# A linear-attention and cosine-gated MLP kernel: POOL's library load, first frames, first loads and planner durations are changed

## The chip, the cores and the metric

The kernel runs on one core of a Trainium2 chip. The metric is the device time of one execution in microseconds (us), median of three runs. The core has a matrix engine (PE, with its weight loads shown as PEld), a vector engine (DVE), a scalar engine (ACT), a general engine (POOL) and a queue engine (SP) that issues the DMA transfers here. Each engine runs its own instructions strictly in the order in which the program lists them, and waits at one whose operands are not ready; what stands behind it waits too.

## The reference

Linear attention over 8 batches of 8 heads with 576 rows of 64, then an MLP whose gate is `h * cos(h)`:

```python
q_s = softmax(q, axis=-1)            # per row, over the 64 values of a head
k_s = softmax(k, axis=2)             # per column, over the 576 rows
kv  = einsum('bhsd,bhse->bhde', k_s, v)
x   = einsum('bhsd,bhde->bhse', q_s, kv)   # -> (4608, 512)
h   = x @ w_in                       # (4608, 2048)
out = (h * cos(h)) @ w_out           # (4608, 512)
```

All of it is float32. The softmaxes subtract the maximum first, as the reference does.

## The kernel before

**Attention.** Heads are taken in pairs; batch `b` has four pairs `p`. For each pair DVE takes a maximum over the rows that lie in one partition (`k_max`, L454), POOL takes it over the 128 partitions with `partition_all_reduce` (`k_all`, L461), DVE subtracts (`k_sub`, L465), ACT takes the exponential (L471) and PE multiplies with `v` (`kv`, L483; 20 matmuls). For q two pairs are handled together, `a` = 0 or 1: `q_max` L553, `q_sub` L556, `q_exp` L560, `q_sum` L564, `q_inv` L568 and L569, `q_norm` L572. PE then transposes q (L595, L599, with the identity `ident`) and multiplies it with kv (L640), which gives x. For batch 0, x is split in high and low parts with the help of a matrix `neg` = -`ident`, which DVE makes (L236) from the identity that POOL makes with a memset and an affine select.

**MLP.** A unit `u` is one block of 512 tokens and one slice `f` of 128 of the 2048 hidden columns; there are 9 x 16 units. PE makes h in 12 matmuls (L746), ACT and DVE make the gate (L752, L756, L762, L766, L770, L774), and PE adds the product with `w_out` into four accumulators (L805, 12 matmuls). h has two buffers, so the h of unit u+2 waits for the gate of unit u (L766). The first eight slices are run for blocks 0 and 1, then the other eight, so every weight slice is needed within the first units of its turn.

**Weights.** They come as raw 64-bit words and are converted before use. One slice of `w_in` or `w_out` costs ACT `bias` L340, `bits` L345, `hi` L364 and DVE `shift` L351, `sign` L357, `lo` L368. A slice pair costs DVE six steps of 128x512.

**Order.** Nothing here is scheduled by the hardware. A `Plan` collects all steps with an engine, a duration written into the code, the tiles read and written and a due time; `Plan.order` simulates in-order engines with those durations in several rounds and returns one order, in which the instructions are then written. So each number in a `plan.add` or `plan.load` is only a cost for the planner; it changes the time through the order alone. `CFG["seq"]` fixes the order of the first loads on SP; `att1` places the due times of batch 1's attention, in units of the MLP.

**Frames.** Some tiles have borders that no load fills: `v_frame` writes ones and zeros around v, `frame` in `load_k` writes -FLT_MAX into the unused half of k's last chunk. POOL does all of them. POOL runs some of its operations from libraries that have to be loaded; the program text shows such a load as a row `ISA` without operands.

```python
ident = const.tile([P, P], F32, name="ident")
make_identity(nc, ident)
neg = const.tile([P, P], F32R, name="neg")
nc.vector.tensor_scalar_mul(neg, ident, -1.0)
```

Of the kernel before, what the change touches and what calls it, by code (L numbers as in the profile page):

```python
# [11 lines left out]
F32 = mybir.dt.float32  # L12
# [175 lines left out]
def linear_attention_then_cos_gated_mlp(  # L188
# [43 lines left out]

    ident = const.tile([P, P], F32, name="ident")
# [20 lines left out]
    def v_frame(t):  # L254
        main, last = v_parts(t)
        nc.gpsimd.memset(main[:, :, 0], 1.0)
        nc.gpsimd.memset(main[:, :, WV - 1], 1.0)
        nc.gpsimd.memset(last[D:P], 0.0)
        nc.gpsimd.memset(last[0:D, :, 0], 1.0)
        nc.gpsimd.memset(last[0:D, :, WL - 1], 0.0)  # L260
        return t
# [9 lines left out]
    plan = Plan()  # L271
    T = {}
# [40 lines left out]
    def load_w(w, f, after=0.0, seq=()):  # L313
# [14 lines left out]
        plan.load(1.46, load, writes=[R], after=after if not seq else 0.0, seq=seq)  # L328

    def convert(w, f):  # L330
# [40 lines left out]
        plan.add("ACT", 0.52, bias, writes=[R])  # L371
        plan.add("ACT", 0.52, bits, writes=[R])
        plan.add("DVE", 0.6, shift, writes=[R])
        plan.add("DVE", 0.6, sign, reads=[R], writes=[c])
        plan.add("ACT", 0.52, hi, reads=[c], writes=[R])
        plan.add("DVE", 0.6, lo, reads=[c], writes=[R])


    def load_k(b, p0, np_, tag, due, seq=()):
# [18 lines left out]
        plan.add("POOL", 0.25, frame, writes=places, due=due)  # L398
# [23 lines left out]
    def load_v(b, p, due, seq=()):  # L422
# [19 lines left out]
        if own:  # L442
            plan.add("POOL", 0.35, frame, writes=place, due=due)
# [3 lines left out]
    def k_steps(b, p, kr, vr, att, due_k, due_kv):  # L447
# [76 lines left out]
        plan.add("DVE", 0.73, k_max, reads=kr, writes=[m1], due=due_k)  # L524
        plan.add("POOL", 1.17, k_all, reads=[m1], writes=[m])
        plan.add("DVE", 0.73, k_sub, reads=[m], writes=kr)
        plan.add("ACT", 0.63, k_exp, writes=kr, table="exp")
# [3 lines left out]
        plan.add("DVE", 0.27, kv_inv, reads=[o], writes=[r])  # L531
        if b < CFG["XF"]:
            plan.add("POOL", 0.14, kv_frame, writes=[kvw], due=due_kv)
            plan.add("ACT", 0.4, kv_f32, reads=[o, r], writes=[kvw])
        else:
            plan.add("DVE", 0.33, kv_norm, reads=[o, r], writes=[kvt])
            plan.add("ACT", 0.2, kv_hi, reads=[kvt], writes=[kvw])
            plan.add("DVE", 0.2, kv_lo, reads=[kvt], writes=[kvw])
        return kvw

    def q_steps(b, a, place, due):
# [32 lines left out]
        plan.add("DVE", 1.27, q_max, reads=qr, writes=[qm], due=due)  # L574
        plan.add("DVE", 1.27, q_sub, reads=[qm], writes=qr)
        plan.add("ACT", 1.06, q_exp, writes=qr, table="exp")
        plan.add("DVE", 1.27, q_sum, reads=qr, writes=[qs])
        plan.add("DVE", 0.34, q_inv, writes=[qs])
        plan.add("DVE", 1.27, q_norm, reads=[qs], writes=qr)

    def x_steps(b, p, place, kvw, tq, tx, due_q, due_x):
# [403 lines left out]
```

## Time and profile before

| what | value |
|---|---|
| median of three runs | 916.33 us (915.85 to 916.66) |
| the profiled execution | 915.42 us, of which the span from first to last instruction is 913.6 us |
| PE busy | 867.9 us, 95% |
| DVE busy | 565.4 us, 62% |
| ACT busy | 508.6 us, 56% |
| POOL busy | 41.3 us, 5% |

Busy shares are means over the whole span. The first and last stretches differ from the rest, so the stretches have to be read apart: where PE is not busy, time is lost that PE cannot win back, since later on it is busy without a gap.

### The profile page before, as it was taken

To read this page: it belongs to the slowest core of one execution; us is meant where nothing else is said; L and a number is where in the kernel's file an instruction comes from. 1 tells how busy PE (TensorE), PEld (TensorE's weight loads), DVE (VectorE), ACT (ScalarE), POOL (GpSimd) and SP (SyncE) were. 2 spreads that over 40 slices of the span, in tenths; PEclk is the share of its full clock that TensorE was granted. 3 is DMA by queue.
4 is the path that set the end of the run, shared out by engine and by line. 5 is a ranking of instruction groups with operands and counts; after the bars stand their busy time and mean duration, and the time that the engine had idled before them with its cause. 6 is when DMAs were issued, how large, how long until landed. Compare 5 with 4: busy or idle time off the path is not lost.

```text
span 913.6 us, 11913 instructions
## 1 busy us (share of the span) xinstructions
PE 867.9 (95%) x4440; PEld 715.4 (78%) x4440; DVE 565.4 (62%) x920; ACT 508.6 (56%) x900; POOL 41.3 (5%) x84
## 2 busy tenths in 40 slices
PE   0579999999999999999999999999999999999997
PEld 0457888888888888888888888888888888888885
DVE  2998968997558654776477556845574444333332
ACT  2699778876436545574646555565563353334332
POOL 1120100000100010000000000000000000000000
PEclk9999999999999999999999999999999999999999
DMA  8573164423032011311140004100300020001001
GB/s 241 170 226 88 46 211 170 143 66 121 28 111 67 28 28 58 94 28 29 46 105 30 28 21 129 32 5 25 111 16 4 2 93 1 0 1 47 1 1 46
DMA packets 95801, 61.59 MB, mean 67 GB/s; under 512 B 53760, under 2 KB 86528, under 8 KB 95744
## 3 DMA queue, kind: packets, MB, share of 16 engines
q1 hardware_dynamic: 95744, 60.84, 22.5%
q8 instruction: 35, 0.57, 0.3%
q14 instruction: 22, 0.18, 0.1%
HBM read 48.23 MB, written 12.58 MB: 67 GB/s over the span
## 4 chain that ended last, share of the span: by engine, by line
PE 87%; DVE 6%; ACT 3%; SPq 2%; DMA 1%; issue 1%; POOL 0%; ACTq 0%; DVEq 0%
PE acc L805 41%; PE h L746 41%; PE x_False L640 2%; PE kv L483 2%; PE qt L595 1%; DVE m L454 1%; DVE k L465 1%; DMA raw_i<-in_moe_w_in_dram 1%; DMA k<-in_k_dram 1%; ACT L762 0%; ACT q L560 0%; SPq L415 0%; DVE glo L774 0%; DVE w_o L368 0%; DVE kt L766 0%
## 5 line engine op out<-in xcount | busy, mean ns | idle before, releaser
L746 PE MATMUL h<-x,w_i 128*128 128x512 f32 x1536 | 374.7, 393 | 3.3 <-DVE kt L766 3.0
L805 PE MATMUL acc<-w_o,ghi 128*128 128x512 f32 x1152 | 358.4, 392 | 0.0
L746 PEld LDWEIGHTS h<-x,w_i 128*128 128x128 f32 x1536 | 287.1, 189 | 64.6 <-DVE kt L766 3.8
L805 PEld LDWEIGHTS acc<-w_o,ghi 128*128 128x128 f32 x1152 | 213.4, 188 | 42.8
L805 PE MATMUL acc<-w_o,glo 128*128 128x512 f32 x576 | 224.5, 390 | 0.0
L756 DVE SCALAR_TENSOR_TENSOR kt<-kt,h 128x512 f32<-128x512 int32 x144 | 98.7, 686 | 142.2 <-ACT kt L752 142.0
L752 ACT ACTIVATE kt<-h 128x512 int32<-128x512 f32 x144 | 86.1, 598 | 178.2 <-PE h L746 178.0
L766 DVE TENSOR_TENSOR kt<-kt,h 128x512 f32<-128x512 f32 x144 | 98.6, 685 | 76.9 <-ACT kt L762 75.6
L770 ACT CAST ghi<-kt 128x512 fp32r<-128x512 f32 x144 | 89.5, 622 | 83.6 <-DVE kt L766 63.5
L774 DVE TENSOR_TENSOR glo<-kt,ghi 128x512 fp32r<-128x512 f32 x144 | 99.8, 693 | 56.5 <-ACT ghi L770 56.0
L805 PEld LDWEIGHTS acc<-w_o,glo 128*128 128x128 f32 x576 | 108.1, 188 | 23.3
L762 ACT ACTIVATE kt<-kt 128x512 f32<-128x512 f32 x144 | 91.3, 635 | 52.4 <-DVE kt L756 51.6
L483 PE MATMUL kv<-v_sb,k 128*64 128x66 f32 (+1 forms) x600 | 22.8, 231 | 28.7 <-ACT k L471 28.7
L483 PEld LDWEIGHTS kv<-v_sb,k 128*64 128x64 f32 x600 | 20.0, 143 | 34.7 <-ACT k L471 29.4
L746 PE MATMUL h<-x_l,w_i 128*128 128x512 f32 x192 | 46.1, 389 | 0.0
L454 DVE TENSOR_REDUCE m<-k 128x128 f32<-128x640 f32 x32 | 41.6, 1300 | 2.2 <-POOL m L461 1.5
L746 PEld LDWEIGHTS h<-x_l,w_i 128*128 128x128 f32 x192 | 36.0, 188 | 7.5
L762 ACT ACT_TABLE_LOAD x30 | 38.5, 1283 | 0.5
L461 POOL PARTITION_ALL_REDUCE m<-m x32 | 32.7, 1022 | 134.1 <-DVE m L454 126.5
L640 PE MATMUL x_False<-qt,kvw 128*128 128x288 f32 x176 | 34.6, 324 | 2.3 <-ACT qt L623 2.3
L640 PEld LDWEIGHTS x_False<-qt,kvw 128*128 128x128 f32 x176 | 28.7, 193 | 6.8 <-issue 3.1
L465 DVE TENSOR_TENSOR k<-k,m 128x640 f32<-128x640 f32 x32 | 26.5, 835 | 11.1 <-POOL m L461 11.1
(76 smaller groups left out, 550.7 us busy)
## 6 DMA issues: line engine op xcount, KB each, us to landing
raw_i<-in_moe_w_in_dram SPq DMA_DIRECT2D x16, 512.0 KB, 6.0
raw_o<-in_moe_w_out_dram SPq DMA_DIRECT2D x16, 512.0 KB, 5.4
q<-in_q_dram SPq DMA_DIRECT2D x32, 256.0 KB, 3.6
out_dram<-o SPq DMA_DIRECT2D x32, 256.0 KB, 2.3
v_sb<-in_v_dram SPq DMA_DIRECT2D x30, 256.0 KB, 3.4
k<-in_k_dram SPq DMA_DIRECT2D x14, 512.0 KB, 3.9
part<-o SPq DMA_DIRECT2D x8, 256.0 KB, 2.2
o<-part SPq DMA_DIRECT2D x8, 256.0 KB, 2.8
```

The source lines that it names most:

```text
L454: nc.vector.tensor_reduce(out=t.rearrange("p (h d) -> p h d", h=2), in_=T["k", b, p].rearrange("p h c d -> p h d c"), axis=AX.X, op=ALU.max,)
L465: nc.vector.tensor_sub(t, t, x.rearrange("p (h o d) -> p h o d", h=2, o=1).broadcast_to([P, 2, NC, D]))
L483: nc.tensor.matmul(x[h * D : (h + 1) * D, odd : odd + vt.shape[1]], t[:, h, c, :], vt, start=(c == CM), stop=(c == CM - 1),)
L640: nc.tensor.matmul(t[:, 0:HALF], a, c[:, cs], start=(n == 0), stop=(n == len(parts) - 1 and not again))
L746: nc.tensor.matmul(o, a, x, start=(c == 0 and n == 0), stop=(c == KC - 1 and n == 2))
L752: nc.scalar.activation(t, T["h", u], AF.Identity, bias=0.25, scale=1.0 / TWO_PI)
L756: nc.vector.scalar_tensor_tensor(t.bitcast(F32), t, -TWO_PI, T["h", u], op0=ALU.mult, op1=ALU.add)
L762: nc.scalar.activation(t, t, AF.Sin, bias=0.5 * math.pi)
L766: nc.vector.tensor_mul(t, t, T["h", u])
L770: nc.scalar.copy(t, T["kt", u].bitcast(F32))
L774: nc.vector.tensor_sub(t, T["kt", u].bitcast(F32), T["gh", u].bitcast(F32))
L805: nc.tensor.matmul(T["acc", j], a[:, js], w, start=(first and n == 0), stop=(last and n == 2))
```

## The change

Five edits, in the order of the program:

- Before the identity is made, DVE fills a 128x1 tile with ones and POOL runs one `partition_all_reduce` on it, whose result nobody uses. It is now POOL's first operation that needs a library.
- All frames of v, and those of k for batch 0, are written by DVE instead of POOL.
- The planner is told that POOL is taken for its first 9 us.
- The first loads come in another order: q of the first two pairs first, the first slice of `w_out` last of this list instead of second.
- Nearly all planner durations of DVE, ACT, PE and the weight loads are replaced, most of them by larger ones, and the due times of batch 1's attention are moved from units 1.29 to 3.26 to units 2.5 to 6.5.

```diff
-    att1=(1.29, 3.26),
+    att1=(2.5, 6.5),
...
     seq=[
-        ("i", 0), ("o", 0), ("v", 0), ("k", 0), ("q", 0), ("q", 1), ("k", 1), ("k", 2),
-        ("v", 1), ("q", 3), ("k", 3), ("q", 2), ("v", 2), ("v", 3),
+        ("q", 0), ("q", 1), ("k", 0), ("i", 0), ("k", 1), ("v", 0), ("q", 2), ("q", 3),
+        ("k", 2), ("v", 1), ("k", 3), ("v", 2), ("v", 3), ("o", 0),
     ],
...
+    ones, warm = (vp.tile([P, 1], F32, name=f"first{i}") for i in range(2))
+    nc.vector.memset(ones, 1.0)
+    nc.gpsimd.partition_all_reduce(warm, ones, P, RED.max)
     ident = const.tile([P, P], F32, name="ident")
     make_identity(nc, ident)
...
     def v_frame(t):
         main, last = v_parts(t)
-        nc.gpsimd.memset(main[:, :, 0], 1.0)
...
+        nc.vector.memset(main[:, :, 0], 1.0)
...
     plan = Plan()
+    plan.add("POOL", 9.0, None)
...
-            nc.gpsimd.memset(t[D:P, :, CM, :], -FLT_MAX)
+            (nc.gpsimd if b else nc.vector).memset(t[D:P, :, CM, :], -FLT_MAX)
...
-        plan.add("DVE", 0.73, k_max, reads=kr, writes=[m1], due=due_k)
-        plan.add("POOL", 1.17, k_all, reads=[m1], writes=[m])
+        plan.add("DVE", 1.28, k_max, reads=kr, writes=[m1], due=due_k)
+        plan.add("POOL", 1.05, k_all, reads=[m1], writes=[m])
```

Some thirty more lines change a duration in the same way.

The lines of the changed kernel are numbered five or six higher. On POOL the start of the program reads as follows in the kernel before, from the identity's memset to the first two all-reduces (L461) of batch 0; `v_sb` and `v` are v tiles, `kvw` the weights for x:

```order
masks.py:197 MEMSET ident 128x128
L256 MEMSET v_sb_83 128x4
L257 MEMSET v_sb_83 128x4
L258 MEMSET v_sb_83 64x132
masks.py:199 ISA
masks.py:199 AFFINE_SELECT ident<-ident 128x128
...
L506 MEMSET kvw_3_200 128x128
L461 ISA
L461 ISA m_0_226<-m_0_0_221 128x128
L461 ISA m_1_260<-m_0_1_244 128x128
```

In the changed kernel it is this, whole:

```order
masks.py:197 MEMSET ident 128x128
L512 MEMSET kvw_0_177 128x128
L237 ISA
L237 ISA first_73<-first_72 128x1
masks.py:199 AFFINE_SELECT ident<-ident 128x128
L512 MEMSET kvw_1_179 128x128
L512 MEMSET kvw_2_183 128x128
L512 MEMSET kvw_3_185 128x128
L467 ISA m_0_224<-m_0_0_218 128x128
L467 ISA m_1_241<-m_0_1_234 128x128
```

The rows without operands (masks.py:199 ISA and L461 ISA before, L237 ISA now) are the library loads: two before, one now. The first memset of kvw stands ahead of it, and no frame is filled on POOL here any more.

On DVE the first work behind the memsets of the start was this in the kernel before, as far as the first `k_sub` (L465) and what follows it; raw and wc are a weight slice in conversion, w its result:

```order
L351 SCALAR_TENSOR_TENSOR raw_i_168<-raw_i_168 128x512
L357 SCALAR_TENSOR_TENSOR wc_i_213<-raw_i_168 128x512
L351 SCALAR_TENSOR_TENSOR raw_o_176<-raw_o_176 128x512
L236 TENSOR_SCALAR neg<-ident 128x128
L454 TENSOR_REDUCE m_0_0_221<-k_0_170 128x128
L368 TENSOR_TENSOR w_i_219<-wc_i_213,w_i_219 128x512
L357 SCALAR_TENSOR_TENSOR wc_o_228<-raw_o_176 128x512
L465 TENSOR_TENSOR k_0_170<-k_0_170,m_0_226 128x640
L368 TENSOR_TENSOR w_o_232<-wc_o_228,w_o_232 128x512
L553 TENSOR_REDUCE qm_0_240<-q_0_205 128x18
```

In the changed kernel, behind 28 memsets:

```order
L559 TENSOR_REDUCE qm_0_213<-q_0_172 128x18
L460 TENSOR_REDUCE m_0_0_218<-k_0_175 128x128
L241 TENSOR_SCALAR neg<-ident 128x128
L562 TENSOR_TENSOR q_0_172<-q_0_172,qm_0_213 128x1152
L357 SCALAR_TENSOR_TENSOR raw_i_207<-raw_i_207 128x512
L471 TENSOR_TENSOR k_0_175<-k_0_175,m_0_224 128x640
L460 TENSOR_REDUCE m_0_1_234<-k_1_181 128x128
L570 TENSOR_REDUCE qs_0_239<-q_0_172 128x18
L559 TENSOR_REDUCE qm_1_256<-q_1_215 128x18
```

`neg` (L241) now stands ahead of the first `q_sub` (L562), and the conversion of the first weights has moved behind the attention of batch 0.

Later on DVE, where the k of batch 1 is first touched, the kernel before had other work between the two maxima (L454) of one load:

```order
L454 TENSOR_REDUCE m_1_0_451<-k_0_378 128x128
L491 TENSOR_SCALAR r_3_466<-kv_3_424 128x1
L494 RECIPROCAL r_3_466<-r_3_466 128x1
L357 SCALAR_TENSOR_TENSOR wc_i_472<-raw_i_266 128x512
L351 SCALAR_TENSOR_TENSOR raw_o_343<-raw_o_343 128x512
L454 TENSOR_REDUCE m_1_1_497<-k_0_378 128x128
```

The changed kernel has:

```order
L363 SCALAR_TENSOR_TENSOR wc_o_420<-raw_o_262 128x512
L497 TENSOR_SCALAR r_3_427<-kv_3_407 128x1
L500 RECIPROCAL r_3_427<-r_3_427 128x1
L460 TENSOR_REDUCE m_1_0_442<-k_0_346 128x128
L460 TENSOR_REDUCE m_1_1_476<-k_0_346 128x128
L357 SCALAR_TENSOR_TENSOR raw_i_268<-raw_i_268 128x512
```

The two maxima share one buffer (`m1` has one), and now stand directly one behind the other; they also stand earlier, ahead of nearly all weight conversions.

On DVE, from the first `k_sub` (before) or the first `q_sub` (now) up to the `lo` of the seventh slice of `w_in` (f = 6), the same steps stand in another order, but for these: only before, the first `q_max`; only now, three `shift`, `sign` and `lo` of slice 0 of `w_in`, `shift` and `sign` of slice 0 of `w_out`, and `shift` of `w_in` slice 7 and of `w_out` slice 6, seven conversion steps in all. On PE the x of pair 2 of batch 1 (4 matmuls) now stands ahead of the h of unit 6, and before stood behind it. After the first units PE's order differs in a few rows of each batch, up to the last batch of attention; from there to the end the orders of PE, ACT and DVE are the same.

## Rows read from the trace of the kernel before

**Rows 1.** Four stretches: us; PE, PEld, DVE, ACT, POOL busy (count); PEclk, DMA share, GB/s.

```profile
0.00:23.08 23.08, 0.00 (x1) 0.00 (x1) 6.60 (x13) 5.73 (x8) 4.28 (x35) 1.00 0.87 241
21.43:96.00 74.57, 56.72 (x358) 43.46 (x359) 69.55 (x108) 62.67 (x129) 9.22 (x14) 0.98 0.56 159
96.17:121.94 25.77, 25.53 (x131) 20.42 (x129) 22.86 (x38) 19.20 (x35) 4.28 (x5) 1.00 0.19 59
121.94:907.00 785.06, 785.06 (x3952) 651.35 (x3952) 467.86 (x766) 420.77 (x729) 23.56 (x30) 1.00 0.18 54
```

**Rows 2.** POOL in order of time, 0 to 40 us: start, duration, what [idle before].

```profile
1.08 0.20 POOL L258 MEMSET v_sb<- 64x132 f32 x1
...
10.19 0.28 POOL masks.py:199 TENSOR_SCALAR_AFFINE_SELECT ident<-ident 128x128 f32<-128x128 f32 x1 [8.90 <-issue]
...
13.12 0.34 POOL L506 MEMSET kvw<- 128x128 f32 x2
20.67 0.72 POOL L461 PARTITION_ALL_REDUCE m<-m  x1 [7.21 <-issue]
25.36 1.73 POOL L461 PARTITION_ALL_REDUCE m<-m  x1 [3.97 <-DVE m L454]
```

**Rows 3.** DVE in order of time, the rows around three places.

```profile
10.50 0.23 DVE L236 TENSOR_SCALAR neg<-ident 128x128 fp32r<-128x128 f32 x1 [2.71 <-POOL ident masks.py:199]
11.33 1.24 DVE L454 TENSOR_REDUCE m<-k 128x128 f32<-128x640 f32 x1 [0.60 <-POOL k L388]
...
21.43 0.83 DVE L465 TENSOR_TENSOR k<-k,m 128x640 f32<-128x640 f32 x1 [7.53 <-POOL m L461]
...
22.77 1.35 DVE L553 TENSOR_REDUCE qm<-q 128x18 f32<-128x1152 f32 x1
24.04 1.23 DVE L454 TENSOR_REDUCE m<-k 128x128 f32<-128x640 f32 x1
...
71.79 0.68 DVE L756 SCALAR_TENSOR_TENSOR kt<-kt,h 128x512 f32<-128x512 int32 x1
72.39 0.69 DVE L351 SCALAR_TENSOR_TENSOR raw_i<-raw_i 128x512 int32<-128x512 int32 x1
...
95.32 0.68 DVE L368 TENSOR_TENSOR w_i<-wc_i,w_i 128x512 fp32r<-128x512 f32 x1
```

**Rows 4.** PE in order of time: the first kv, x of batches 0 and 1, h of units 6 and 10.

```profile
23.08 1.36 PE L483 MATMUL kv<-v_sb,k 128*64 128x66 f32 x20 [23.08 <-ACT k L471]
...
36.97 2.26 PE L640 MATMUL x_False<-qt,kvw 128*128 128x288 f32 x4 [1.84 <-ACT qt L623]
...
91.97 1.13 PE L640 MATMUL x_False<-qt,kvw 128*128 128x288 f32 x4
92.72 0.84 PE L805 MATMUL acc<-w_o,ghi 128*128 128x512 f32 x2
...
96.17 3.02 PE L746 MATMUL h<-x,w_i 128*128 128x512 f32 x12
...
121.94 3.06 PE L746 MATMUL h<-x,w_i 128*128 128x512 f32 x12 [0.24 <-DVE kt L766]
```

**Rows 5.** The chain that ended last: one unit's h at full pace (start, us, what).

```profile
146.76 2.72 PE h L746 x12
```

**Rows 6.** One DMA issue on SP in order of time.

```profile
3.26 0.60 SPq L393 DMA_DIRECT2D k<-in_k_dram  x1
```

**Rows 7.** Busy time in three stretches of 10 us; columns as in rows 1.

```profile
10.00:20.00 10.00, 0.00 (x0) 0.00 (x0) 2.75 (x4) 0.62 (x1) 2.86 (x26) 1.00 0.85 225
20.00:30.00 10.00, 2.58 (x40) 2.33 (x40) 7.94 (x10) 3.88 (x7) 2.82 (x3) 1.00 0.74 207
50.00:60.00 10.00, 9.57 (x74) 7.21 (x75) 9.93 (x15) 9.22 (x24) 3.19 (x5) 1.00 0.76 241
```

**Rows 8.** DMA issues, 25 to 60 us: what, count, KB each, median us to landing.

```profile
k<-in_k_dram SPq DMA_DIRECT2D x2, 512.0 KB, 4.7
```

**Rows 9.** ACT in order of time: the first exponential of k.

```profile
22.29 0.74 ACT L471 ACTIVATE k<-k 128x640 f32<-128x640 f32 x1 [7.69 <-DVE k L465]
```

More of the change, by code (lines that the diff above doesn't have):

```diff
@@ L255, in v_frame @@
         main, last = v_parts(t)
-        nc.gpsimd.memset(main[:, :, 0], 1.0)
[L257 to L260, printed above, removed]
+        nc.vector.memset(main[:, :, 0], 1.0)
+        nc.vector.memset(main[:, :, WV - 1], 1.0)
+        nc.vector.memset(last[D:P], 0.0)
+        nc.vector.memset(last[0:D, :, 0], 1.0)
+        nc.vector.memset(last[0:D, :, WL - 1], 0.0)
         return t
@@ L326, in load @@
                 )
-        plan.load(1.46, load, writes=[R], after=after if not seq else 0.0, seq=seq)
+        plan.load(1.66, load, writes=[R], after=after if not seq else 0.0, seq=seq)
     def convert(w, f):
@@ L370, in convert @@
         c = ring("wc")
[L371 to L376, printed above, removed]
+        plan.add("ACT", 0.67, bias, writes=[R])
+        plan.add("ACT", 0.65, bits, writes=[R])
+        plan.add("DVE", 0.68, shift, writes=[R])
+        plan.add("DVE", 0.68, sign, reads=[R], writes=[c])
+        plan.add("ACT", 0.62, hi, reads=[c], writes=[R])
+        plan.add("DVE", 0.69, lo, reads=[c], writes=[R])
     def load_k(b, p0, np_, tag, due, seq=()):
@@ L396, in load @@
             nc.sync.dma_start(t[0:NL, :, CM, :], src[:, NM:S, :].rearrange("h p d -> p h d"))
-        plan.add("POOL", 0.25, frame, writes=places, due=due)
+        plan.add("POOL" if b else "DVE", 0.25, frame, writes=places, due=due)
         plan.load(0.91 * np_, load, writes=places, due=due, parts=2, seq=seq)
@@ L442, in load_v @@
         if own:
-            plan.add("POOL", 0.35, frame, writes=place, due=due)
+            plan.add("DVE", 0.45, frame, writes=place, due=due)
         plan.load(0.91, load, writes=place, due=due, parts=2, seq=seq)
@@ L572, in q_norm @@
             nc.vector.tensor_mul(rows(), rows(), over_d(T["qs", b, a]))
[L574 to L579, printed above, removed]
+        plan.add("DVE", 1.35, q_max, reads=qr, writes=[qm], due=due)
+        plan.add("DVE", 1.35, q_sub, reads=[qm], writes=qr)
+        plan.add("ACT", 1.16, q_exp, writes=qr, table="exp")
+        plan.add("DVE", 1.35, q_sum, reads=qr, writes=[qs])
+        plan.add("DVE", 0.44, q_inv, writes=[qs])
+        plan.add("DVE", 1.35, q_norm, reads=[qs], writes=qr)
     def x_steps(b, p, place, kvw, tq, tx, due_q, due_x):
@@ L697, in x_steps @@
             plan.add(
-                "ACT" if twice else "DVE", (0.37, 0.3)[i] - 0.08 * twice, lambda i=i: x_lo(i),
+                "ACT" if twice else "DVE", (0.45, 0.38)[i] - 0.04 * twice, lambda i=i: x_lo(i),
                 reads=[o, xr[2 * i]], writes=[xr[2 * i + 1]],
@@ L858, in out_rows @@
             plan.load(0.73, fetch, reads=[("part", b, j)], writes=[s])
-            plan.add("DVE", 0.6, take, reads=[acc[j]], writes=[s])
+            plan.add("DVE", 0.69, take, reads=[acc[j]], writes=[s])
         else:
-            plan.add("ACT", 0.48, take, reads=[acc[j]], writes=[s])
+            plan.add("ACT", 0.59, take, reads=[acc[j]], writes=[s])
         plan.load(0.73, put, reads=[s], writes=[("part", b, j)] if cont else [])
```

50 lines of the change are left out of this document (25 added, 25 removed).

## Prediction

> **What bounds the kernel now.** I read the busy time by stretches first. From 121.94 us to 907 us PE is busy 785.06 of 785.06 us, in a stretch in which DVE is busy 60% and ACT 54% [rows 1]. The chain of work that ended last runs through PE alone there, one unit's 12 matmuls in 2.72 us [rows 5]. So nothing that the planner does there is worth anything unless it opens a gap, and what a change wins or loses is how early PE reaches that unbroken stretch. Its first matmul, the kv of pair 0, starts at 23.08 us [rows 4]: all of the first 23.08 us is lost to PE, at a DMA share of 0.87. Between 21.43 and 96.00 us DVE is busy 69.55 of 74.57 us, ACT 62.67 and PE 56.72 [rows 1]: DVE sets the pace of this stretch, and PE follows it. At 96.00 us DVE ends the `lo` of the seventh w_in slice (95.32 + 0.68) [rows 3] and at 96.17 PE begins the h of unit 6 with it [rows 4]. From there PE has nearly no gap (25.53 of 25.77 us) [rows 1].
>
> Then the order of time on POOL and DVE shows what fills the first 23 us. POOL is idle for 8.90 us ahead of the identity's affine select and 7.21 us ahead of its first all-reduce, both put down to "issue", that is, to nothing it waited for [rows 2]. These are the places of the two rows of library loading. All frames come behind the first gap; so DVE's first maximum over k, at 11.33 us, waited for POOL's frame of k, and the first subtraction of k, at 21.43 us, waited 7.53 us for the all-reduce behind the second gap [rows 3]. The exponential follows at 22.29 [rows 9] and kv at 23.08.
>
> **Term 1: the start of the DVE stretch.** POOL reaches its one library load when the identity's memset and one memset of kvw are done; before, as many small memsets ended at 1.28 us (1.08 + 0.20) [rows 2], and the list is shorter now, so 1.1 us. The load costs between 7.2 us (the gap before the same operation, later in the program) and 8.9 us (the gap at the same place, for another operation) [rows 2]. The one is the same code, the other the same moment, so I take the middle, 8.05: done at 9.15, bounds 8.3 to 10.0. The idle all-reduce over one column takes 0.72 us as the shortest row near has it, or up to 1.0 (the rows of all 32 have a mean of 1.02, one here 1.73) [rows 2]; I take 0.85. The affine select 0.28 and `neg` 0.23 follow. `neg` now stands ahead of the first `q_sub` on DVE, so that one starts at 9.15 + 0.85 + 0.28 + 0.23 = 10.5 us, bounds 9.5 and 11.5. What stands ahead of `neg`, 28 memsets, `q_max` 1.35 and `k_max` 1.24, is hidden below this as long as the first q and k have landed: SP issues one DMA in 0.60 us and a little [rows 6], so that k, fifth and sixth, is issued by 4 us; with 4.7 us to landing [rows 8] it is there by some 8.5, and its maximum is done by 9.8. The memsets cost nothing under the wait for these loads; without that cover they would cost some 3 us.
>
> The Trainium skill ("GPSIMD Engine Reference", section 2.1) says that the first call of a freshly loaded kernel pays about 6 us for loading, with no instruction in the profile to show it. The trace agrees on the invisible gap and not on its size, 7.21 and 8.90 us; by 6 us, `neg` would wait for the k maximum instead, the first `q_sub` would start near 10.0, and the total would come out 0.5 us lower than mine.
>
> The all-reduce of pair 0 is on time: POOL is free of the affine select at 10.3, three memsets of kvw take 0.5 (two took 0.34 [rows 2]) and the all-reduce 0.72 to 1.0, so 11.5 to 11.8; DVE reaches `k_sub` at 10.5 + 1.27 + 0.60 = 12.4. The first kv then starts at 12.4 + 0.83 + 0.74 + gaps, 14.1 us, against 23.08.
>
> **Term 2: the DVE stretch itself.** From the first `k_sub` (before) or the first `q_sub` (now) to the `lo` of w_in slice 6 DVE has the same steps but for the first `q_max`, which is gone from it, and seven conversion steps of 128x512, which are new in it. Back to back, `q_max` takes 1.27 us (22.77 to 24.04) and a step of 128x512 0.60 (71.79 to 72.39) [rows 3]. So the stretch takes 74.57 - 1.27 + 7 x 0.60 = 77.5 us, if its waits are as before (74.57 - 69.55 = 5.0 us [rows 1]). It ends at 10.5 + 77.5 = 88.0 against 96.00: 8.0 us earlier.
>
> **Term 3: waits that are new in it.** The two k maxima of one load of batch 1 stand back to back and share a buffer, so the second waits for POOL's all-reduce: 0.72 to 1.73 us, I take 1.0. The first of them stands earlier in DVE's row than before: by the steps ahead of it DVE is there at about 31.5 us (21 us after the first `q_sub`). Its load cannot be issued until the second transpose of batch 0's q has left the tile, which by the chain q_norm, transposes, kv, x ends at about 25.5; SP issues it behind the store of the first x_left, at about 26. Landing 4.7 us later [rows 8] it would be in time. But the queue is deep: 8.4 MB (12 loads of q, k, v of 0.295 MB, seven weight slices of 0.52, two v and this k) come up to and with this load. In the first 20 us transfers ran at 225 to 241 GB/s [rows 1, 7], which was all that SP's issue asked for; at 50 to 60 us 241 GB/s came at a share of 0.76, that is, 317 at full share [rows 7]. With 241 GB/s from 2.2 us, where the first bytes come, to 18.5, where the weights are next (3.9 MB), and the rest at 317: 18.5 + 4.5 / 0.317 = 32.7. Between landing in time and this I take a wait of 1.0 us; bounds 0 and 7 (233 GB/s throughout: 2.2 + 8.4 / 0.233 = 38.3).
>
> **Term 4: PE.** It has the x of pair 2 of batch 1 behind it when unit 6 begins; before, that came after. 0.75 us (91.97 to 92.72) [rows 4]. Between units 6 and 10 PE took 25.77 us for eight times 12 matmuls, two x, one kv and one transpose, 8 x 2.72 + 2 x 0.75 + 1.2 = 24.5 at full pace; what of the 1.3 is won back I leave in the range.
>
> The new durations of the planner, apart from the order, run on no engine and cost nothing. Behind unit 10 they move a few rows of PE per batch, beside an unbroken PE: nothing, while DVE and ACT have over a third of the stretch free. Without that cover a gap costs what it is long.
>
> **Sum.** 8.0 - 1.0 - 1.0 + 0.75 = 6.8 us earlier. The profiled execution took 915.42 us (913.6 of span and 1.8 around it); 908.6 with the change. The median is 0.9 above that execution, so 916.33 - 6.8 = **909.5 us**.
>
> **Rivals.**
> *The transfers give the lead back.* The weights and the k of batch 1 are now asked for some ten us earlier, behind the same loads. Speaking for it: a share of 0.85 to 0.87 in the first 23 us already. Against it: between 21.43 and 96 us the share is 0.56 [rows 1]. At a wait of 2 to 5.5 us in place of 1.0 the gain is 5.8 to 2.3: 910.5 to 914.0 us.
> *The waits shrink too.* Batch 0's q is normalized before any weight is converted, so the first x, at 36.97 us before [rows 4], could come some 14 us earlier (10.5 + 8.5 for the rows to `q_norm`, then 3 for transposes and kv); if half of the 5.0 us of DVE waits and the 1.3 of PE go with it and no new ones come, the gain is 9 to 12: 904.3 to 907.3.
> *The change doesn't do what it says.* If the affine select needed a library of its own at run time, 7.2 to 8.9 us more would stand ahead of `neg`, and DVE with everything behind it: a gain of -0.4 to -2.1, 916.7 to 918.4, no change or just more. The program shows no second load there.
> *Slower: the load of batch 1's k is the new head of the chain.* DVE stops in its row at that maximum, with almost all weight conversions behind it. Each us beyond 31.5 + 1.0 costs one. It eats the gain of 6.8 when k lands at 39.3, and decides for slower by over 0.2% (1.8 us) at 41.1, which means a mean of 8.4 / (41.1 - 2.2) = 216 GB/s up to there. The stretches at 225 and 207 [rows 7] are on both sides of that, but neither had a full queue. At 207 it lands at 42.8: 3.5 slower, 919.8.
>
> **How the numbers follow.** I give the forecast (gain 5.8 to 9) 0.55, the transfers giving back 0.20, the waits shrinking 0.13, no effect 0.05, slower 0.07. 0.2% is 1.8 us, about what a measurement of this kernel can tell from no change. Faster is the first three: 0.88. The forecast's own range is 907.3 to 910.5. The range for 8 in 10 reaches into both neighbours: 904.5 to 914.0, which leaves out the last two cases and the far end of the third.
>
> **What would show it.** Right: one idle gap of POOL of 7.2 to 8.9 us near 1 to 10 us and none ahead of the all-reduce of batch 0; `neg` at 9.3 to 11.3; first kv at 13 to 15.5; the w_in `lo` of slice 6 ending near 89; PE without a gap from about there. Wrong: DVE idle for several us at batch 1's first k maximum, released by a DMA; a second POOL gap ahead of the affine select; or PE gaps after unit 10 that were not there.

## The result and the profile after

| | before | after |
|---|---|---|
| median | 916.09 us (915.27 to 916.66, 4 runs) | 908.08 us (907.75 to 910.19, 4 runs) |
| profiled execution | 915.42 us, span 913.6 | 907.75 us, span 906.0 |
| ratio after to before | | 0.9918, 95% interval 0.9901 to 0.9935 |

The change makes the kernel faster by 8.0 us (medians) or 7.7 us (profiled executions); the forecast was 6.8. The number came out, but one price inside its first term, the 8.05 us of the library load, was wrong by its whole size, and the wait for batch 1's k was wrong by 3.6 us the other way.

Busy time in four stretches of the changed kernel, with the columns of [rows 1]:

```profile
0.00:13.55 13.55, 0.00 (x1) 0.00 (x1) 8.04 (x35) 4.27 (x5) 3.46 (x12) 1.00 0.76 195
8.67:89.76 81.09, 59.81 (x365) 44.02 (x365) 72.21 (x114) 66.49 (x138) 11.37 (x15) 0.94 0.64 193
89.76:114.20 24.44, 24.44 (x125) 19.76 (x125) 23.20 (x36) 18.53 (x35) 3.08 (x4) 1.00 0.38 112
114.20:906.00 791.80, 785.53 (x3953) 651.17 (x3951) 464.22 (x767) 419.01 (x726) 21.18 (x31) 1.00 0.18 53
```

From unit 10 to the end the kernel takes 791.80 us, before 913.6 - 121.94 = 791.66: nothing changed there. All of the gain lies ahead of unit 10. DVE's stretch to unit 6 has 81.09 - 72.21 = 8.9 us of idle time where it had 5.0 [rows 1].

POOL in order of time in the changed kernel, answering [rows 2]:

```profile
0.89 0.20 POOL L512 MEMSET kvw<- 128x128 f32 x1
1.23 0.36 POOL L237 PARTITION_ALL_REDUCE first<-first  x1
1.47 0.36 POOL masks.py:199 TENSOR_SCALAR_AFFINE_SELECT ident<-ident 128x128 f32<-128x128 f32 x1
...
8.72 1.86 POOL L467 PARTITION_ALL_REDUCE m<-m  x1 [6.46 <-DVE m L460]
```

The gap of 7 to 9 us that was to be left is not there at all. The first all-reduce runs at 1.23 us, and POOL's next idle time has a releaser: it waits for DVE.

DVE in order of time, the rows that answer to [rows 3] and the two that wait longest behind them:

```profile
8.54 0.21 DVE L241 TENSOR_SCALAR neg<-ident 128x128 fp32r<-128x128 f32 x1
8.67 1.35 DVE L562 TENSOR_TENSOR q<-q,qm 128x1152 f32<-128x1152 f32 x1
11.30 0.69 DVE L357 SCALAR_TENSOR_TENSOR raw_i<-raw_i 128x512 int32<-128x512 int32 x1 [1.27 <-ACT raw_i L351]
11.91 0.82 DVE L471 TENSOR_TENSOR k<-k,m 128x640 f32<-128x640 f32 x1
...
35.63 1.29 DVE L460 TENSOR_REDUCE m<-k 128x128 f32<-128x640 f32 x1 [4.59 <-DMA k<-in_k_dram]
37.76 1.29 DVE L460 TENSOR_REDUCE m<-k 128x128 f32<-128x640 f32 x1 [0.83 <-POOL m L467]
...
89.53 0.69 DVE L374 TENSOR_TENSOR w_i<-wc_i,w_i 128x512 fp32r<-128x512 f32 x1
```

The first k subtraction comes 9.52 us earlier (21.43 to 11.91). Then DVE stands 4.59 us at batch 1's first k maximum. SP issued that k at 27.99 us, and loads of this size took 7.0 us to land (issue on SP; issues from 20 to 40 us with the columns of [rows 8]):

```profile
27.99 0.38 SPq L399 DMA_DIRECT2D k<-in_k_dram  x1
```

```profile
k<-in_k_dram SPq DMA_DIRECT2D x2, 512.0 KB, 7.0
```

What is left at the `lo` of w_in slice 6 is 5.8 us (96.00 to 90.22). PE, answering [rows 4]; the h rows are a quarter of unit 0 and those of units 2, 6 and 10:

```profile
13.55 1.35 PE L489 MATMUL kv<-v_sb,k 128*64 128x66 f32 x20 [13.55 <-ACT k L477]
...
21.14 2.29 PE L646 MATMUL x_False<-qt,kvw 128*128 128x288 f32 x4
...
42.49 1.65 PE L752 MATMUL h<-x,w_i 128*128 128x512 f32 x3
...
55.22 4.70 PE L752 MATMUL h<-x,w_i 128*128 128x512 f32 x12 [5.47 <-DVE kt L772]
...
89.76 3.08 PE L752 MATMUL h<-x,w_i 128*128 128x512 f32 x12 [0.17 <-DVE kt L772]
...
114.20 2.88 PE L752 MATMUL h<-x,w_i 128*128 128x512 f32 x12
```

The first kv is 9.53 us earlier, the first x 15.8, unit 6 6.41 and unit 10 7.74. Of the lead of 9.5 us at the start a third is lost by unit 6, and a little is won back behind it.

The 12 matmuls of unit 2 took 4.70 us behind 5.47 us without work, those of unit 10 took 2.88. The windows show where PE's clock was lower, and what filled the time before:

```profile
20.00:30.00 10.00, 9.52 (x74) 6.95 (x76) 9.86 (x17) 8.43 (x21) 2.57 (x4) 1.00 1.03 332
30.00:40.00 10.00, 8.02 (x50) 5.12 (x46) 4.32 (x7) 7.13 (x23) 2.08 (x4) 1.00 1.08 374
...
42.00:46.00 4.00, 3.82 (x37) 2.74 (x34) 4.00 (x6) 3.35 (x7) 1.49 (x1) 0.60 0.48 107
50.00:60.00 10.00, 4.78 (x14) 3.79 (x15) 10.00 (x16) 9.54 (x15) 0.00 (x0) 0.66 0.59 180
```

From 20 to 40 us the transfers run at a full share, and from 30 to 40 us DVE is busy only 4.32 of 10 us. The granted clock has a mean of 0.60 from 42 to 46 us and of 0.66 from 50 to 60 us, that is, the engine stood on the lower of its two levels, 1.2 GHz instead of 2.4, for a part of each. What the second costs is not new. Unit 2 was as slow in the kernel before:

```profile
66.39 4.62 PE L746 MATMUL h<-x,w_i 128*128 128x512 f32 x12 [2.48 <-DVE kt L766]
```

New is the first: three matmuls of unit 0, a quarter of it, took 1.65 us there, and its quarters took 0.96 to 1.08 us in the kernel before.

### The profile page after: what moved, and what is told of

It is laid out like the page before. It is cut to its first block, busy times and chain, and to the rows that moved or that the text cites. A ratio compares the mean times of both kernels' runs of the same rounds, so it can differ in the third digit from the quotient of the medians.

```text
span 906.0 us, 11877 instructions
## 1 busy us (share of the span) xinstructions
PE 869.8 (96%) x4440; PEld 714.9 (79%) x4440; DVE 564.1 (62%) x945; ACT 505.3 (56%) x898; POOL 37.2 (4%) x61
## 4 chain that ended last, share of the span: by engine, by line
PE 89%; DVE 4%; SPq 2%; DMA 2%; issue 1%; ACT 0%; POOL 0%; DVEq 0%; POOLq 0%
PE acc L811 42%; PE h L752 42%; PE x_False L646 2%; PE kv L489 2%; PE qt L601 1%; DMA v_sb<-in_v_dram 1%; DMA k<-in_k_dram 1%; SPq L421 0%; DVE m L460 0%; SPq L417 0%; DVE wc_i L363 0%; DVE k L471 0%; DMA q<-in_q_dram 0%; DVE w_o L374 0%; POOL m L467 0%
## 5 line engine op out<-in xcount | busy, mean ns | idle before, releaser
L768 ACT ACT_TABLE_LOAD x29 | 37.2, 1283 | 0.5
L467 POOL PARTITION_ALL_REDUCE m<-m x32 | 30.6, 956 | 121.9 <-DVE m L460 121.9
L624 ACT CAST qt<-qt 128x512 fp32r<-128x512 f32 (+1 forms) x36 | 15.4, 465 | 21.6 <-PE qt L601 21.6
```

The source lines that it names most:

```text
L467: nc.gpsimd.partition_all_reduce(t, T["m1", b, p], P, RED.max)
L768: nc.scalar.activation(t, t, AF.Sin, bias=0.5 * math.pi)
```

## The experiments

The theory after the first look (A in most of the expectations): the gain is the start without POOL's two gaps, carried to unit 6 by DVE's full row, less what DVE then waits for batch 1's k. The rival was that the loads' order and the planner's new numbers do it. A second question was why the one library load that is left costs nothing.

Two numbers go with each run: PE's idle time in the first 130 us (130 less PE's busy time in that window) and the mean granted clock in the same window. Each ratio is to runs of the kernel before that were timed beside it: their median was 914.52 us for e1 to e4, 915.00 for e5 to e8 and 915.77 for e9 to e12, so runs of different groups are compared by their ratios.

| kernel | median us | ratio to before (95%) | PE idle to 130 us | clock to 130 us |
|---|---|---|---|---|
| before | 916.09 | | 39.5 | 0.99 |
| after | 908.08 | 0.9918 (0.9901 to 0.9935) | 30.0 | 0.96 |
| e1 library part alone | 904.94 | 0.9893 (0.9878 to 0.9908) | 28.7 | 0.99 |
| e2 after, old numbers | 907.84 | 0.9924 (0.9912 to 0.9937) | 30.1 | 0.96 |
| e3 after, two loads | 908.30 | 0.9928 (0.9914 to 0.9941) | 31.8 | 0.96 |
| e4 after, iota at the end | 907.15 (one run) | | 29.6 | 0.96 |
| e5 after, k early | 908.67 | 0.9928 (0.9916 to 0.9941) | 31.1 | 0.95 |
| e6 after, old first loads | 906.05 | 0.9899 (0.9884 to 0.9914) | 31.7 | 0.97 |
| e7 frames alone | 912.13 | 0.9969 (0.9958 to 0.9981) | 37.2 | 0.99 |
| e8 replanned | 905.45 | 0.9895 (0.9881 to 0.9908) | 27.2 | 0.96 |
| e9 after, second xl | 909.85 | 0.9940 (0.9925 to 0.9955) | 30.9 | 0.93 |
| e10 e5 with second xl | 906.78 | 0.9907 (0.9890 to 0.9923) | 30.9 | 0.99 |
| e11 after, late weights | 907.12 | 0.9910 (0.9895 to 0.9924) | 28.5 | 0.97 |
| e12 e8 with second xl | 905.86 | 0.9895 (0.9880 to 0.9910) | 27.6 | 0.96 |

**e1: the library part alone.**

```diff
+    ones, warm = (vp.tile([P, 1], F32, name=f"first{i}") for i in range(2))
+    nc.vector.memset(ones, 1.0)
+    nc.gpsimd.partition_all_reduce(warm, ones, P, RED.max)
     ident = const.tile([P, P], F32, name="ident")
```

> The kernel before with the idle all-reduce ahead of the identity, and nothing else: old numbers, old order of the first loads, frames on POOL. Theory A (the whole gain is a start without POOL's two gaps, of 8.90 and 7.21 us, carried to unit 6 by DVE's full row, less what DVE then waits for batch 1's first k): no gap of 7 to 9 us on POOL; the first k subtraction when k has landed, its maximum and the all-reduce are done, at 10.5 to 12 us instead of 21.43; of these 9.5 to 11 us 2 to 6 are lost again to transfers, so 4 to 8 us faster than before, 908 to 912 us. Theory B (the gain hangs on the loads' new order and on the planner's new numbers, the library part alone gives little, since the first k and q come behind two weight slices): under 3 us faster, 913 us or more. PE unbroken from unit 6 on in both.

Three lines won 9.6 us by medians, 914.52 less 904.94, where the whole change won 8.0 (ratios 0.9893 and 0.9918, whose intervals just overlap). DVE's and PE's rows in order of time:

```profile
10.68 0.81 DVE L468 TENSOR_TENSOR k<-k,m 128x640 f32<-128x640 f32 x1
...
36.25 1.30 DVE L457 TENSOR_REDUCE m<-k 128x128 f32<-128x640 f32 x1
```

```profile
85.47 3.02 PE L749 MATMUL h<-x,w_i 128*128 128x512 f32 x12
...
111.22 3.06 PE L749 MATMUL h<-x,w_i 128*128 128x512 f32 x12 [0.22 <-DVE kt L769]
```

Against the kernel before the first k subtraction is 10.75 us earlier, unit 6 10.70, unit 10 10.72 [rows 3, 4], the span 10.4. The row of before has moved as a block. The new waits that theory A charged here, 2 to 6 us, did not come: batch 1's k maximum starts at 36.25 without a wait, since this order has eight conversion steps of DVE between 26 and 36 us where the changed kernel has three. The maximum itself is no earlier than in the changed kernel (35.63); what differs is how much of the later work is done ahead of it. Theory A's best case, 908 us, was 3 us short; theory B falls.

**e2: the planner's old numbers.** The changed kernel with the old durations, old due times of batch 1 and without POOL's 9 us.

```diff
-    att1=(2.5, 6.5),
+    att1=(1.29, 3.26),
...
-    plan.add("POOL", 9.0, None)
```

> The changed kernel with the planner's old durations, the old bounds for batch 1 and no 9 us of POOL; the first all-reduce, the frames on DVE and the new order of the loads stay. Theory A: the new numbers are worth nothing for the start; they set how many conversion rows DVE has ahead of batch 1's first k maximum. By its order five more of them stand ahead of it here, about 3 us of the 4.6 us that DVE waits there in the changed kernel: 905 to 908 us, the same as the changed kernel's 908.1 or 1 to 3 us faster. Theory B (durations of the trace give the planner a better order): 909.5 to 913 us, slower than the changed kernel by 1.5 us or more.

907.84 us, the same as the changed kernel: the new numbers are worth nothing that can be measured. The wait for k is gone, which is more than was expected, but DVE stands instead behind ACT, 1.33 us for w_out's `hi` and 1.80 for w_in's:

```profile
31.95 0.69 DVE L371 TENSOR_TENSOR w_o<-wc_o,w_o 128x512 fp32r<-128x512 f32 x1 [1.33 <-ACT w_o L367]
...
36.55 0.69 DVE L371 TENSOR_TENSOR w_i<-wc_i,w_i 128x512 fp32r<-128x512 f32 x1 [1.80 <-ACT w_i L367]
```

e1 and e2 were timed beside the same runs of before, and their intervals do not overlap: given the library part, frames on DVE and the new order of loads together cost 2.9 us.

**e3: two loads again.** The changed kernel without its idle all-reduce.

```diff
-    ones, warm = (vp.tile([P, 1], F32, name=f"first{i}") for i in range(2))
-    nc.vector.memset(ones, 1.0)
-    nc.gpsimd.partition_all_reduce(warm, ones, P, RED.max)
```

> The changed kernel without its idle all-reduce, so that POOL again needs a library for the affine select and another for the all-reduces. Theory A (the libraries cost what the gaps show and stand on the path): gaps of about 8.9 us ahead of the affine select and 7.2 us ahead of the first all-reduce; first k subtraction near 19 us instead of 11.91; of these 7 us DVE gives back up to 3 at the wait for batch 1's k (4.6 us now), so 4 to 7 us slower than the changed kernel: 912 to 915 us. Theory B (the gain came from the order of loads and the planner): within 1.5 us of the changed kernel, 907 to 909.5 us.

POOL, and DVE at the first k subtraction and batch 1's first k maximum:

```profile
8.40 0.28 POOL masks.py:199 TENSOR_SCALAR_AFFINE_SELECT ident<-ident 128x128 f32<-128x128 f32 x1 [7.31 <-issue]
...
15.56 0.72 POOL L464 PARTITION_ALL_REDUCE m<-m  x1 [6.43 <-issue]
```

```profile
16.31 0.83 DVE L468 TENSOR_TENSOR k<-k,m 128x640 f32<-128x640 f32 x1 [4.16 <-POOL m L464]
...
35.94 1.28 DVE L457 TENSOR_REDUCE m<-k 128x128 f32<-128x640 f32 x1 [0.81 <-DMA k<-in_k_dram]
```

Both gaps are back and the first k subtraction is 4.4 us late, yet the time is within 0.1% of the changed kernel's. At batch 1's k maximum DVE is 0.31 us behind it: its wait there fell from 4.59 to 0.81. All other instructions stand in the changed kernel's order. In this order, 4.4 us of the start are worth next to nothing, because the landing of that k decides: taken out of the whole change, the library part costs nothing that can be measured. Theory B's number came, for theory A's reason: the gaps stand where they were expected, and the k wait absorbs them, by 3.8 us where "up to 3" was granted.

**e4: another library at the end.** One iota behind everything, whose output nobody uses.

```diff
+        last = vp.tile([P, 1], I32, name="last")
+        nc.gpsimd.iota(last, pattern=[[0, 1]], base=0, channel_multiplier=1)
```

> The changed kernel with one more instruction on POOL behind all others, an iota over one column, for which POOL must load the first library; its output is used by nobody. Theory A (in the changed kernel the all-reduce's library is still there from the execution before, and so its load costs nothing): now each execution begins with the other library, and a gap of 7 to 9 us stands ahead of the first, idle all-reduce, which ends near 9 to 10 us; first q subtraction near 10.5 us instead of 8.67, first k subtraction 12 to 12.5 instead of 11.91; time 907.5 to 909.5 us, since DVE waits for raw_i and batch 1's k anyway. Theory B (a load that stands first is hidden behind the start of the program or costs nothing): no gap, the first q subtraction at 8.6 to 8.8 us, time as the changed kernel.

```profile
7.23 0.38 POOL L237 PARTITION_ALL_REDUCE first<-first  x1 [6.17 <-issue]
...
8.90 1.88 POOL L467 PARTITION_ALL_REDUCE m<-m  x1 [0.60 <-DVE m L460]
...
622.70 0.13 POOL L959 IOTA last<- 128x1 int32 x1 [6.93 <-issue]
```

Now the gap is there, 6.17 us ahead of the very instruction that ran at 1.23 us in the changed kernel, and 6.93 us ahead of the iota. So the load costs nothing in the changed kernel because the library is still there from the execution before; the kernel before used two in turn and had to load both each time. Theory A is shown for the gap. Its size of 6.17 us is below the range that I took from [rows 2]. At this size `neg` waits for the k maximum and not for POOL: it starts at 8.71 us, 0.17 later than without the gap, and the first k subtraction is only 0.03 later:

```profile
11.94 0.82 DVE L471 TENSOR_TENSOR k<-k,m 128x640 f32<-128x640 f32 x1
```

The Trainium skill ("GPSIMD Engine Reference", section 2.1) gives about 6 us for the first call of a freshly loaded kernel; 6.17 us agrees with it, and the other gaps of these runs, 6.43 to 9.40 us, are longer. One run, 907.15 us: no loss that it could show.

**e5: k ahead in the queue.** On SP only, five transfers change places: w_in 3, v(1,1), w_out 2, the store of x_left and k(1,0) in the changed kernel, and now k(1,0) ahead of the other four. The helper that finds the loads is left out here.

```diff
+    moved = [
+        load_of("load_k", (1, 0)), load_of("w", ("i", 3)), load_of("load_v", (1, 1)), load_of("w", ("o", 2))
+    ]
...
+    steps = [i for i in first if i not in moved] + moved + [i for i in steps[at + 1 :] if i not in moved]
```

> The changed kernel with one thing moved on SP: the load of batch 1's first k stands right behind the weights of w_out slice 1, ahead of w_in slice 3, the second v of batch 1, w_out slice 2 and the first store of x_left, which follow it in their old order. Theory A (the wait for this load, 4.6 us in the changed kernel, is what keeps it behind the kernel with the library part alone): k issued as soon as POOL has written its frame, near 24.8 us instead of 28; DVE waits under 1 us for it; its pair's second maximum then waits for POOL, whose row has a frame and a memset of kvw ahead of the all-reduce that end at 33.4 us, so it starts near 34.3 instead of 37.76: 2 to 3.5 us faster than the changed kernel, 904.5 to 906.5 us. Theory B (other waits stand right behind this one, so that its length doesn't decide): the first maximum comes early, and units 2 to 6 at the same times as in the changed kernel; 907 to 909 us.

DVE and ACT:

```profile
32.37 1.27 DVE L460 TENSOR_REDUCE m<-k 128x128 f32<-128x640 f32 x1 [0.25 <-DMA k<-in_k_dram]
...
39.06 0.69 DVE L357 SCALAR_TENSOR_TENSOR raw_i<-raw_i 128x512 int32<-128x512 int32 x1 [2.62 <-ACT raw_i L351]
```

```profile
35.99 0.21 ACT L663 COPY xl<-x_False 128x64 f32<-128x64 f32 x1 [3.16 <-DMA x_left<-xl]
```

The wait for k is gone and the time is not. The store of x_left went out 3.16 us later (30.57 instead of 27.41), ACT stood behind it, and DVE behind ACT. Theory B's outcome, through a wait that neither named: with one buffer for xl, the later store cost here what the earlier load had won. PE's clock has a part in the time too: units 2 and 4 took 5.49 and 4.62 us (4.70 and 3.38 in the changed kernel).

**e6: the old order of first loads** in the changed kernel.

```diff
-        ("q", 0), ("q", 1), ("k", 0), ("i", 0), ("k", 1), ("v", 0), ("q", 2), ("q", 3),
+        ("i", 0), ("o", 0), ("v", 0), ("k", 0), ("q", 0), ("q", 1), ("k", 1), ("k", 2),
```

> The changed kernel with the first loads in the order of the kernel before: w_in and w_out slice 0 first, then v, k, q. Library, frames on DVE, new planner's numbers stay. Theory A (the new order is the part that costs: with the weights first, DVE has conversions to do while q and k come, and reaches batch 1's k with work behind it): 904 to 906.5 us, near the 904.9 of the library part alone. Theory B (the new order is what gives q and k early, and the planner's new numbers cost): 909 to 912 us, slower than the changed kernel.

906.05 us, in theory A's range; 0.0019 below the changed kernel, with intervals that overlap a little. Together with e2 it points to a new order that costs and does not gain. Neither run shows that alone: this interval overlaps, and e2 differs from e1 in the frames too. The estimates are 1.7 us (from e6) and at most 2.9 (from e2).

**e7: the frames alone,** on the kernel before.

```diff
-        nc.gpsimd.memset(main[:, :, 0], 1.0)
+        nc.vector.memset(main[:, :, 0], 1.0)
...
-            nc.gpsimd.memset(t[D:P, :, CM, :], -FLT_MAX)
+            (nc.gpsimd if b else nc.vector).memset(t[D:P, :, CM, :], -FLT_MAX)
```

> The kernel before with one part of the change, the first frames on DVE; two libraries as before, old order, old numbers. Theory A (POOL's second gap begins when POOL reaches the first all-reduce; the frames between the two gaps held it back): the second gap follows the affine select at once, first k subtraction at 16.5 to 18.5 us instead of 21.43, and DVE's full row carries this to unit 6: 3 to 5 us faster than before. Theory B (26 memsets on POOL cost what they take, some 2 us, beside waits): under 1 us faster.

POOL's gaps were 9.40 us ahead of the affine select and 6.54 ahead of the all-reduce at 17.75; the first k subtraction came at 18.51 us, 2.92 earlier than before, and the kernel was 0.31% faster, 2.9 us: just short of theory A's 3 to 5 us, and theory B falls. The start's lead went one to one into the total here too.

```profile
18.51 0.82 DVE L465 TENSOR_TENSOR k<-k,m 128x640 f32<-128x640 f32 x1 [5.01 <-POOL m L461]
```

**e8: replanned.** Library and frames as in the changed kernel, the planner's old durations without POOL's 9 us, batch 1 later, a longer landing, and another order of the first loads.

```diff
-    att1=(2.5, 6.5),
+    att1=(3.5, 5.5),
...
-        return self.LAT.get((a[0], b[0]), 1.0 if a[0] == "BUS" else 0.2)
+        return self.LAT.get((a[0], b[0]), 2.2 if a[0] == "BUS" else 0.2)
```

> Library first and frames on DVE as in the changed kernel, with the planner's old durations; it is told that a transfer lands 2.2 us behind its last byte instead of 1.0, batch 1 is due later (3.5, 5.5), and the first loads come as w_in 0, k 0, q 0, q 1, v 0, k 1, w_out 0, then as in the changed kernel. Theory A (what is lost in the changed kernel behind the start are waits of DVE for transfers that the planner takes for landed): DVE waits under 1 us for batch 1's k, has its first conversion before 6 us, and unit 6 begins at 81 to 84 us: 900.5 to 904 us. Theory B (ACT or PE bounds the stretch to unit 6 as soon as DVE doesn't): 904.5 to 908 us, with DVE's idle time behind ACT.

DVE waits no more for batch 1's k, and PE's idle time is the least of all, 27.2 us; but unit 6 begins at 88.30 us and not at 81 to 84, and the time is e1's and in theory B's range. DVE does wait for ACT, three times between 31 and 37 us, 1.02 us at the longest. What the order won in idle time against e1, 1.5 us, is not in the time, and PE's matmuls were slower: the granted clock from 50 to 60 us was 0.51, and unit 2's 12 matmuls took 5.49 us (4.60 in e1).

```profile
54.36 5.49 PE L748 MATMUL h<-x,w_i 128*128 128x512 f32 x12 [2.45 <-DVE kt L768]
```

**e9 to e12: a second buffer for xl,** alone (e9), with e5's order (e10) and in e8's plan (e12); e11 changes two planner numbers instead. In e9 and e10 the planner is not told of the buffer, so that its order stays.

```diff
-        x4k=8, kq=2, qm=1, qs=2, ql=1, m1=1, m=2, r=2, kvt=1, kvw=4, xl=1, stage=2, wc=1, r2=3, ghi=2,
+        x4k=8, kq=2, qm=1, qs=2, ql=1, m1=1, m=2, r=2, kvt=1, kvw=4, xl=2, stage=2, wc=1, r2=3, ghi=2,
...
```

> The changed kernel with a second buffer for xl, the tile whose store to x_left ACT waits for; every engine's order is the changed kernel's. In the changed kernel ACT waits 1.62 and 1.12 us for these stores at 33.4 and 39.7 us, while DVE waits 4.59 us for batch 1's k. Theory A (k's late landing, not the store, holds DVE in the changed kernel): ACT's two waits go and DVE's stays; 907 to 908.5 us, as the changed kernel. Theory B (the store is part of what holds DVE): 1 us or more faster, under 907 us.

ACT's waits for the store are gone, DVE's for k is 4.24 us: theory A. But 909.85 us is outside its range, with every engine's order the same (the ratio's interval still overlaps that of the changed kernel). In the profiled executions, 2.9 us apart, the difference is in PE's clock: the 12 matmuls of unit 1 took 3.88 us and those of unit 4 5.67 (2.92 and 3.38 in the changed kernel), the mean to 130 us is 0.93.

```profile
35.55 1.31 DVE L460 TENSOR_REDUCE m<-k 128x128 f32<-128x640 f32 x1 [4.24 <-DMA k<-in_k_dram]
```

```profile
48.09 3.88 PE L752 MATMUL h<-x,w_i 128*128 128x512 f32 x12
...
75.39 5.67 PE L752 MATMUL h<-x,w_i 128*128 128x512 f32 x12
```

> Both together: batch 1's first k loaded ahead of the same four transfers as in e5, and a second buffer for xl, so that the store, which comes later for that, keeps nobody waiting. In e5 DVE waited 0.25 us for k and yet the time stayed, with ACT 3.16 us behind the store and DVE 2.62 us behind ACT. Theory A (two waits stand behind each other, for k and for the store; only with both gone is the lead kept): DVE's waits between 31 and 41 us come to under 2.5 us (5.4 in the changed kernel), units 2 to 6 start 2 to 3.5 us earlier: 904 to 906 us. Theory B (POOL's and PE's rows hold the second maximum anyway, and DVE's row behind it is set by ACT's conversions): 907 us or more.

```profile
31.30 1.27 DVE L460 TENSOR_REDUCE m<-k 128x128 f32<-128x640 f32 x1
34.46 1.30 DVE L460 TENSOR_REDUCE m<-k 128x128 f32<-128x640 f32 x1 [1.88 <-POOL m L467]
35.68 0.68 DVE L357 SCALAR_TENSOR_TENSOR raw_i<-raw_i 128x512 int32<-128x512 int32 x1
```

With the wait for this k and the one for the store gone, DVE's idle time between 31 and 41 us is 3.0 us (5.4 in the changed kernel, under 2.5 expected). DVE is at the raw_i step 3.28 us earlier than in the changed kernel (38.96 there) and unit 6 begins 3.1 us earlier, at 86.64. The time is 906.78 us, 0.8 above theory A's range: of the 3.1 us, which are still there at unit 10, 1.1 are lost behind it, most of them at one wait of PE:

```profile
120.32 3.01 PE L752 MATMUL h<-x,w_i 128*128 128x512 f32 x12 [0.92 <-DVE kt L772]
```

Against e9, which has the same buffers and was timed beside the same runs of before, the intervals do not overlap: 3.1 us faster. Against the changed kernel (0.9907 and 0.9918) the difference is not resolved.

> The changed kernel with two of the planner's numbers altered: weights may be asked for 20 us ahead of their unit instead of 28.78, and a transfer lands 2.2 us behind its last byte instead of 1.0. By its order three weight slices stand ahead of batch 1's first k on SP's queue behind w_in 0 (w_out 0, w_in 1 and 2) instead of six. Theory A (the wait for this k comes from the weights ahead of it in a full queue): 1.6 MB less ahead, at 330 to 370 GB/s 4.2 to 4.8 us: DVE waits under 1 us for k; 903.5 to 906 us. Theory B (k lands late because it is issued late, when batch 0's q has left its tile): wait of 3 us or more as now, 907 us or more.

```diff
-    wwin=28.78,
+    wwin=20,
...
-        return self.LAT.get((a[0], b[0]), 1.0 if a[0] == "BUS" else 0.2)
+        return self.LAT.get((a[0], b[0]), 2.2 if a[0] == "BUS" else 0.2)
```

```profile
30.65 1.28 DVE L460 TENSOR_REDUCE m<-k 128x128 f32<-128x640 f32 x1 [1.21 <-DMA k<-in_k_dram]
```

The k maximum starts five us earlier than in the changed kernel, so the weights ahead of that k did hold it. They held its issue: SP issued it at 23.06 us instead of 27.99, and DVE's wait for it ends 7.6 us behind the issue in both. The time is 907.12 us, which is theory B's. The planner's new order puts other rows behind it: unit 6 begins at 89.14, 0.6 us earlier than in the changed kernel, and the granted clock is 0.66 from 50 to 60 us.

> The replanned kernel of e8 with a second buffer for xl, known to the planner. Theory A (what keeps e8 at the time of the library part alone are ACT's waits and the lower granted clock behind PE's idle time at 50 to 60 us, 0.51 there): with a free ACT row PE's idle time before 130 us falls from 27.2 to 25 to 26.5 us and the clock there is higher: 902 to 904.5 us, the fastest of all. Theory B (e8's stores keep nobody waiting, ACT's row shows none of these waits): as e8, 904.8 to 906.2 us.

905.86 us, as e8: theory B. ACT had none of these waits in e8 to lose.

The fastest kernels are e1, e8, e12 and e6, which these runs do not tell apart. e1 is the kernel before with three lines more.

## Why the prediction was right, step by step

- **Its own signs.** The number is right; the signs that were named for it are mixed. The POOL gap of 7.2 to 8.9 us did not come and `neg` started at 8.54 us, ahead of its 9.3 to 11.3; the first kv (13.55), the missing gap ahead of batch 0's all-reduce and PE's unbroken row did come. And one of the signs named for "wrong" came: DVE idle for several us at batch 1's first k maximum, released by a DMA.
- **Term 1, the start: wrong by the load.** The step "the load costs between 7.2 us and 8.9 us" measured 0: the library was resident (e4). First q subtraction 8.67 us (forecast 10.5, bounds 9.5 to 11.5), set by q's landing and the maxima; first k subtraction 11.91 (12.4), first kv 13.55 (14.1). The bounds came from two rows of the same program, and both rows were of loads that replace another library; that there might be nothing to replace was not among the cases. The idle all-reduce took 0.36 us (0.85 taken).
- **Term 2, the stretch: right in its work, short in its waits.** Forecast 77.5 us with 5.0 of waits, plus 2.0 of term 3: 79.5. Measured from 8.67 to 90.22: 81.5. DVE's idle time to unit 6 is 8.9 us instead of 7.0, so its busy time is the 72.5 us of the forecast within 0.2.
- **Term 3, the new waits: the k wait mis-sized.** 1.0 us was taken, bounds 0 and 7; it was 4.59. DVE was there at 31.04 as forecast (31.5), the k was issued at 27.99 instead of 26, and it took 7.0 us to land instead of the 4.7 of [rows 8], in a queue that moved 374 GB/s at a full share. The two maxima that share a buffer: 0.83 (1.0).
- **Terms 1 to 3 together: two errors that cancel.** 1.83 us too late at the start, 2.0 too short on the way; the `lo` of w_in slice 6 ended at 90.22 us, forecast 88.0 + 2.0 = 90.0. In the forecast that is luck: its sum lets every us of the start into the total, and nothing in it ties the one error to the other. In the kernel the start does not count one to one: a load of 6.17 us moves the first k subtraction by 0.03 us (e4), and a start 4.4 us later is taken up by the k wait (e3).
- **Term 4, PE: 1.33 us** (25.77 to 24.44 between units 6 and 10) for the 0.75 with 0 to 1.3 more.
- **Sum:** 5.8 at the `lo`, 6.4 at unit 6's first matmul, which starts just ahead of that `lo`, and 1.3: 7.7 us, forecast 6.8.
- **What the sum left out: PE's clock.** Idle time before 130 us fell by 9.6 us (39.53 to 29.95), the span by 7.6. The rest went into PE's busy time, which rose by 1.9 us, from 867.9 to 869.8. Some 1.3 of it are three rows between 41 and 46 us (two kv and a quarter of unit 0, 3.9 us where the same rows took 2.7 before); unit 2, slow in both kernels, adds 0.1.
- **Rivals.** The transfers did give part of the lead back (4.59 lies in that rival's 2 to 5.5 us), from a start that was 1.83 us better. The other waits of DVE shrank, as the second rival had it: 8.9 less 4.59 and 0.83 leaves 3.5 us where 5.0 were taken, and the first x came 15.8 us earlier. Batch 1's k as head of the chain is real: it caps what the start is worth in this order (e3), though far from making the kernel slower.
- **What the parts are worth.** The library part alone 9.6 us, the frames alone 2.9, the change without the library part 6.2 (e3; not told apart from the whole by the ratios), all together 8.0. They do not add, since all of them shorten the same start; the new numbers give nothing that can be measured (e2), and the new order of loads seems to take some back (e2, e6).

Not settled: why the lower clock comes where it does and differs between the traces of two programs with the same order (after and e9), and the share of the frames in the 2.9 us between e1 and e2. A kernel with e1's order and frames on DVE was not run.

## What to carry to other kernels

If POOL's operations can all be served by one library, order them so that the program needs no other: the load then costs nothing in an execution that follows another of the same program, as all measured here do. Before pricing a lead at the start, look for the first wait on a transfer further down the row: a lead that only lengthens that wait was worth nothing (e3), and with other work ahead of the wait the whole lead was kept (e1). And change one part at a time: three lines of this change were worth at least as much as all of it.

## What the runs showed of the hardware

- A library load shows as idle time of POOL with no releaser. Loads that replace another library took 6.17 and 6.93 us (e4), 7.31 and 6.43 (e3), 9.40 and 6.54 (e7), 8.90 and 7.21 [rows 2]; a load of the library that the last execution left shows no gap (after and e1, the all-reduce at 1.23 and 1.43 us).
- Two programs with the same order on every engine (after and e9) differ by 1.8 us in the median, with intervals that overlap, and their traces by 0.03 in PE's mean granted clock over the first 130 us. The same 12 matmuls take 2.88 us at the full clock and up to 5.67 where a part of PE's row fell on the lower level. Idle time of PE stood ahead of the slow rows: 2.48 us before unit 2 (before), 5.47 (after), 1.98 before the kv at 41.46 us (after). It does not tell them apart by itself: unit 4 has 1.65 and 0.81 us of it ahead and 3.38 us in the changed kernel, and 1.95 and 0.81 us ahead and 5.67 us in e9.
- A load of 512 KB took 4.7 us to land (median of two) at a mean DMA share of 0.64 (before, 25 to 60 us), and 7.0 us at a full share (after, 20 to 40 us).
